# Attention with a top-32 mask and a mixture of experts: K and Q of two heads loaded and transposed together, V loaded in two groups, and a new order on every engine

## The chip, the cores and the metric

One NeuronCore of a Trainium2 chip runs the whole program. The metric is device time in microseconds; lower is better. Three runs of the kernel before took 1312.78, 1315.38 and 1315.54 us, and their median is the time before.

## The reference

Eight batches of eight heads, 576 positions, 64 values per head, in float32. Each row of scores keeps its 32 largest entries. The result feeds a mixture of eight experts.

```python
scores = scale * np.matmul(q, k.transpose(0, 1, 3, 2))
kth = np.partition(scores, -top_k, axis=-1)[..., -top_k:-top_k + 1]
scores = np.where(scores >= kth, scores, -1000000000.0)
attn = np.exp(scores - np.max(scores, axis=-1, keepdims=True))
attn = attn / (np.sum(attn, axis=-1, keepdims=True) + 1e-09)
attn_out = np.matmul(attn, v)
...
logits = x @ w_gate
...
h = np.maximum(x[mask] @ w1[e], 0.0)
out[mask] = h @ w2[e]
```

## The kernel before, in words

The attention stage goes over 32 pairs: eight batches, two heads at a time. `prep` brings a pair in, `tile_ops` and `soft` work on its nine tiles of 128 query rows (tile 4 holds the last 64 rows of both heads), `tail`, `values` and `logits` finish it. Several pairs are under way at a time. A mixture-of-experts stage follows, which the change leaves alone.

**Two halves.** The products run in 16-bit floats, so K and Q are each kept as a high and a low half in one buffer (`nk`, `nq`, two of each, used in turn). The high half is made on ACT (lines 349 and 350), the low half on POOL: a scaled copy (354), then the scaled copy less the high half (355). V is split likewise on POOL (342, 345, 346).

**What SP issues for a pair.** SP's queue issues all DMAs of the stage and takes them strictly in its own order. `loads` (lines 335 and 336) brings K, and again Q, in four DMAs: for each head its first 512 rows, then its last 64. `loadv` (340 and 341) does the same for V. `turn` (line 360) transposes one half of K or Q by a DMA, 9 blocks of 128 columns each: `K2`, `K3`, `Q2`, `Q1`, four DMAs.

**The row maxima.** After three tiles a small POOL instruction (`most`, line 462) puts the rows' maxima into a spare column of Q's second buffer half, and a DMA (`q2`, line 463) transposes those three blocks anew over the same place. So there are three such transposes in a pair: the first for tiles 0 to 2, the middle one for 3 to 5, the third for 6 to 8.

**Who reads the transposes.** `scores` (line 407) multiplies Q's halves with K's for a first pass, on which DVE finds the 32nd largest (lines 411 to 438) and ACT makes the masks (425, 443). `again` in `soft` computes the scores a second time, transposed: line 482 reads `K2` and `Q1`, line 483 `K3` and `Q2` with the maxima in it. So line 483 of tiles 3 to 5 needs the middle transpose of line 463. Line 487 is the exponential, 490 and 493 on POOL split its result into halves, 584 multiplies with V.

**What sets the order.** Every operation is handed to a planner (`Loom`) with a number from the table `TAU`, one per operation and tile, plus the pair's number times `PER`. On each engine the operations stand in the order of these numbers; a pair's later operations are dealt between the next pairs' earlier ones. SP is one of these engines, `e="D"`. A `pre` entry is a true dependence, an `order` entry only a place behind another. The planner's costs `d` and `late` don't change the order, which the table fixes. The first pair has a path of its own (`first`), and the last one its own numbers (names with `_`).

Of the kernel before, what the change touches and what calls it, by code (L numbers as in the profile page):

```python
# [190 lines left out]
def attention(tc, q,k,v,w_gate,x_out,L,acc,cuts, pairs,ahead=()):  # L191
    NCH=6
    nc=tc.nc
    CW=576//NCH; NCAND=8*NCH
    with ExitStack() as ctx:
# [31 lines left out]
        def rims():  # L227
# [9 lines left out]
        TAU=dict(s0=[0.7506526,1.3511746,1.8516096,8.2571781,10.1588313,11.5600494,16.7645738,18.766314,20.4677931],  # L237
            s1=[0.8507396,1.4512616,3.0526537,8.3572652,10.2589183,11.7602234,16.8646608,18.866401,20.6679671],
            c0=[-2.8733791,-1.2175335,1.996755,6.8668891,8.425332,10.568191,14.4642983,16.8019626,19.0422243],
            c1=[-2.6785738,-1.0227282,4.6266274,7.2564998,8.71754,12.3214393,15.9253385,17.9707948,19.139627],  # L240
            c2=[-1.4123389,0.6331174,4.431822,7.0616944,9.9837749,12.0292312,14.9513117,18.3604056,20.0162511],
            c3=[-1.3149362,0.3409094,4.139614,7.6461105,9.6915669,10.9578017,14.7565063,17.3863787,19.8214458],
            c4=[-2.1915603,-0.146104,3.6526006,7.1590971,10.0811776,12.2240366,15.8279358,18.5552109,19.4318351],
            c5=[-2.4837684,-0.3409094,3.3603925,7.7435132,9.3993588,11.2500098,16.2175466,18.7500163,20.3084592],
            k0=[-0.9253255,1.3149362,4.7240301,8.2305266,10.6655937,12.71105,16.5097546,19.3344324,20.5032646],
            k1=[-0.0487013,1.8019496,5.0162381,8.5227347,11.1526071,13.1980634,17.0941707,19.6266404,20.990278],
            k2=[0.4383121,2.3863657,5.1136408,9.1071508,11.4448151,13.4902715,17.4837814,19.9188485,21.0876807],
            k3=[0.7305201,3.4577952,5.7954596,9.4967615,12.1266339,13.5876741,18.0681975,20.1136538,21.282486],
            k4=[1.7045469,3.8474059,6.574681,9.8863722,12.418842,14.1720902,18.4578082,20.4058619,21.3798887],
            nt=[8.4307985,9.209026,13.1001638,19.3259842,21.1418485,23.2171219,26.8488505,29.4429423,30.4805791],  # L250
            sg=[8.6902077,11.0248903,14.3972097,20.1042117,22.1794852,23.4765311,27.3676689,29.9617607,30.7399883],
            fl=[4.5292247,5.6006542,7.4513052,11.5422178,13.9772849,15.2435197,20.6006672,21.4772914,21.8669021],
            o0=[4.8542199,7.3563951,9.2580482,13.2615285,16.1640518,17.3650959,22.5696203,24.0709254,24.9717085],
            o1=[5.0543939,7.4564821,9.3581352,14.1623116,16.2641388,17.6653569,23.6705774,24.1710124,25.0717955],
            y8=[4.8214328,6.6720837,8.0357213,13.2954661,14.3668956,16.3149492,21.5746941,21.6720967,22.4513182],
            rl=[11.5437087,14.6566189,16.7318923,22.9577128,23.9953495,25.5518046,30.9993974,31.2588066,32.8152617], mo=[7.2970843,16.7126769,24.7159306],
            q2=[6.355525,15.599925,24.844325], ma=[11.9603974,15.1631817,17.7654439,19.466923,20.7680541,23.7706644,29.1753628,26.9734486,30.8768419],
            mb=[12.4608325,15.4634427,17.9656179,19.667097,21.5687502,23.8707514,29.2754498,28.3746667,30.9769289],
            ag0=[12.7610935,15.8637907,18.466053,19.7671841,21.7689242,23.9708384,29.6757978,28.5748407,31.27719],
            ag1=[13.1614415,16.0639648,18.56614,20.3677061,22.0691852,24.6714474,29.7758848,28.7750148,31.377277],  # L260
            ag2=[13.4617026,16.3642258,18.966488,20.8681411,22.2693593,24.7715344,29.8759718,28.8751018,31.577451],
            ag3=[13.7619636,16.5643998,19.366836,21.0683152,22.3694463,24.8716215,30.0761459,29.0752758,32.077886],
            ex=[21.4012577,23.7359403,26.3300321,28.1458964,28.924124,32.2964434,35.1499444,34.3717168,38.0034454],
            eh=[21.8912528,24.2451509,25.1867102,25.6574898,0,30.8360657,37.4269806,33.6607435,44.0178954],
            el=[22.832812,28.011388,30.3652861,26.5990491,0,33.1899639,39.3100991,40.722438,44.9594546], cu=[46.3717935], tm=[27.4738837], tn=[27.6740577], ta=[27.7741447],
            tb=[27.8742317], te=[33.0746709], th=[31.3068454], tl=[31.777625], tc=[34.4799742], tr=[41.635174],
# [58 lines left out]
        def prep(n):  # L325
# [5 lines left out]
            def loads(nm,src,by=nc.sync):  # L331
                t=io.tile([128,9,64],F32,tag=nm+"n",name=nm+"n")
                for h in range(2):
                    o=(0,5)[h]
                    by.dma_start(out=t[:,o:o+4,:],in_=src[b,2*hp+h,0:512,:].rearrange("(p c) d -> p c d",c=4))
                    by.dma_start(out=t[64*h:64*h+64,4,:],in_=src[b,2*hp+h,512:576,:])
                nat[nm]=t
# [20 lines left out]
            def turn(nm):  # L358
# [3 lines left out]
                if nm=="Q2": P["Q2t"]=t  # L362
# [956 lines left out]
```

## Time and profile before

| | us |
|---|---|
| median of three runs | 1315.38 |
| the profiled execution's own time | 1316.4 |
| its span in the profile | 1314.6 |
| stretch 27 to 135, 135 to 862 (attention) | 108, 727 |
| stretch 862 to 1315 (experts) | 453 |
| PE busy over the span | 1230.4 (94%) |
| DVE busy | 1100.7 (84%) |
| ACT busy | 912.9 (69%) |
| POOL busy | 813.7 (62%) |
| DMA queue of SP, share of 16 engines | 42.9% |

How to read it: the busy shares are means over two stages of unlike make, so they don't tell what a change in one stage is worth. Instructions that only wait or issue a DMA are not busy time. The profiled execution took 1.0 us longer than the median. A DMA is shown twice in a trace: as the time that SP took to issue it, and as the time from issue to landing, when its readers may start.

### The profile page before, as it was taken

The page shows a single profiled execution, that of the slowest core. Times are in us where ns is not written, and L with a number is a line of the kernel's source. Part 1 is how long each engine was busy: PE and PEld are TensorE (multiplying, and loading weights), DVE is VectorE, ACT ScalarE, POOL GpSimd, SP SyncE. Part 2 cuts the span into 40 slices and gives each one's busy share as a digit, 9 for nine tenths or more (in the row PEclk, how much of TensorE's full clock was granted, in tenths as well). Part 3 has the DMA queues.
Part 4 walks back from the last instruction along what each step waited for, and adds up shares of the span by engine and source line. Part 5 has one row for each costly group of instructions (what it writes and reads, how often), then busy time and mean ns, then how long its engine had stood idle before and what let it go on. Part 6 is the DMA issues. An engine that isn't in the chain of part 4 may idle for free.

```text
span 1314.6 us, 43939 instructions
## 1 busy us (share of the span) xinstructions
PE 1230.4 (94%) x16447; PEld 937.3 (71%) x16448; DVE 1100.7 (84%) x5550; ACT 912.9 (69%) x2177; POOL 813.7 (62%) x1054
## 2 busy tenths in 40 slices
PE   8999999999999999999999999968999999999996
PEld 7777777787778777877777787757575665665662
DVE  7999989999999999999999999868999998843320
ACT  4989888998899989999898998714444353444220
POOL 3789788888888988899888988701213223311001
PEclk9999999999999999999999999968999999999998
DMA  5544645445544453653665364014557667672001
GB/s 109 105 90 82 128 95 101 113 103 95 128 81 104 109 115 89 103 139 78 99 134 96 77 140 87 20 47 155 179 186 237 185 157 205 196 201 76 21 17 38
DMA packets 317970, 148.60 MB, mean 113 GB/s; under 512 B 283444, under 2 KB 299828, under 8 KB 316724
## 3 DMA queue, kind: packets, MB, share of 16 engines
q1 hardware_dynamic: 311412, 126.55, 42.9%
q0 software_dynamic: 5888, 18.88, 4.6%
q8 instruction: 130, 2.13, 0.7%
q14 instruction: 92, 0.75, 0.2%
q10 hardware_dynamic: 448, 0.30, 0.1%
HBM read 71.34 MB, written 18.87 MB: 69 GB/s over the span
## 4 chain that ended last, share of the span: by engine, by line
PE 27%; DVE 24%; ACT 18%; issue 13%; DMA 11%; POOL 3%; SPq 1%; POOLq 0%; another core or an unknown queue 0%; ACTq 0%; DVEq 0%
DVE cd L411 8%; DMA Q<-nq 6%; ACT w L425 6%; PE ph L1179 5%; PE ph L1213 4%; DVE st L438 4%; PE pt L477 3%; PE s L428 3%; PE s L407 3%; ACT r L443 2%; PE pv L584 2%; ACT xb L558 2%; ACT F L487 2%; PE pt L483 2%; DMA wr<-in_moe_w_dram 2%
## 5 line engine op out<-in xcount | busy, mean ns | idle before, releaser
L411 DVE MAX8 cd<-s 128x8 f32<-128x96 f32 x1728 | 381.0, 250 | 24.9 <-PE s L407 24.0
L493 POOL TENSOR_TENSOR elm<-F,ehm 128x512 f16<-128x512 f32 x253 | 290.0, 1157 | 10.3
L438 DVE MAX8 st<-s 128x8 f32<-128x584 f32 x288 | 218.5, 768 | 18.2 <-PE s L428 17.0
L425 ACT ACTIVATE w<-s,st 128x576 uint16<-128x576 f32 x288 | 216.3, 751 | 5.8
L443 ACT ACTIVATE r<-s,st 128x576 bf16<-128x576 f32 x288 | 213.5, 753 | 1.2 <-DVE st L438 1.2
L483 PE MATMUL pt<-Q,K 65*128 65x128 f16 (+1 forms) x1280 | 186.2, 215 | 16.5 <-DMA Q<-nq 16.3
L407 PE MATMUL s<-K,Q 128*128 128x192 f16 (+3 forms) x1280 | 194.8, 288 | 3.9 <-DMA Q<-nq 2.8
L1179 PE MATMUL ph<-xT,w1h 128*128 128x288 f16 (+2 forms) x1056 | 191.6, 282 | 0.4 <-issue 0.4
L482 PE MATMUL pt<-Q,K 128*128 128x128 f16 (+1 forms) x1280 | 187.3, 214 | 0.0
L487 ACT ACTIVATE F<-pt 128x512 f32<-128x512 f32 x256 | 155.2, 608 | 18.3 <-PE pt L483 17.2
L1229 POOL DMA_INDIRECT out_dram<-ob,idx x39 | 40.2, 1031 | 203.7 <-ACT ob L1224 186.9
L428 PE MATMUL s<-w,off 128*128 128x384 f16 x576 | 151.7, 284 | 11.7 <-ACT w L425 3.1
L490 POOL TENSOR_SCALAR ehm<-F 128x512 f16<-128x512 f32 x253 | 155.2, 618 | 8.6 <-ACT F L487 8.6
L1179 PE MATMUL ph<-xT,w1l 128*128 128x288 f16 (+2 forms) x528 | 148.1, 282 | 0.0
L1133 POOL DMA_INDIRECT xg<-x,idx x40 | 46.9, 1173 | 150.4 <-DVE idx L1076 47.3
L482 PEld LDWEIGHTS <-K 128*128 128x128 f16 x1280 | 117.0, 98 | 31.3 <-issue 26.6
L584 PEld LDWEIGHTS <-ehm 128*128 128x128 f16 x2024 | 112.5, 98 | 15.1 <-issue 0.5
L483 PEld LDWEIGHTS <-K 65*128 65x128 f16 x1280 | 117.9, 98 | 4.1
L584 PE MATMUL pv<-vl,ehm 128*128 128x65 f16 x1012 | 118.9, 193 | 0.0
L584 PE MATMUL pv<-vh,ehm 128*128 128x65 f16 x1012 | 118.6, 194 | 0.1
L584 PE MATMUL pv<-vh,elm 128*128 128x65 f16 x1012 | 118.6, 193 | 0.0
L477 PEld LDWEIGHTS <-r 128*128 128x128 bf16 x1280 | 86.0, 97 | 42.8 <-issue 30.6
(297 smaller groups left out, 3370.1 us busy)
## 6 DMA issues: line engine op xcount, KB each, us to landing
wr<-in_moe_w_dram SPq DMA_DIRECT2D x32, 1024.0 KB, 6.8
kn<-in_k_dram SPq DMA_DIRECT2D x64, 128.0 KB, 2.7
vt<-in_v_dram SPq DMA_DIRECT2D x64, 128.0 KB, 2.8
x<-xb SPq DMA_DIRECT2D x8, 1024.0 KB, 5.0
qn<-in_q_dram SPq DMA_DIRECT2D x62, 128.0 KB, 2.3
Q<-nq SPq DMA_TRANSPOSE x160, 2.9
kn<-in_k_dram SPq DMA_DIRECT2D x64, 16.0 KB, 2.2
K<-nk SPq DMA_TRANSPOSE x64, 3.3
```

Source lines behind the costliest of these rows:

```text
L407: x=T.matmul(s_ps[rows,S0+a:S0+b_],P[Q][:,qc],P[K][:,h*576+a:h*576+b_],start=(Q=="Q1"),stop=(Q=="Q2"))
L411: x=V.max(D["cd"][:,c*8:c*8+8],D["s"][:,S0+CW*c:S0+CW*(c+1)])
L425: A.activation(D["w"],D["s"][:,S0:S0+576],AF.Sign,bias=P["st"][:,i,32:33],scale=(1+2.0**-21),accum_out=acc[:,col])
L428: x=T.matmul(D["s"][:,S0+a:S0+b_],off,P["w"][i][:,a:b_],start=False,stop=True,skip_group_check=True)
L438: def next8(): V.max(P["st"][:,i,24:32],D["s"][:,S0-8:S0+576])
L443: A.activation(r,D["s"][:,S0:S0+576],AF.Relu,bias=P["st"][:,i,31:32],scale=-1.0)
L482: T.matmul(o,K2[:,kb:kb+128],Q1[:,qc],start=False,stop=False,skip_group_check=True)
L483: T.matmul(o,K3[0:65,kb:kb+128],Q2[0:65,qc],start=False,stop=(c==3 and h==sub[-1][0]),skip_group_check=True)
L487: A.activation(D["E"],D["pt"],AF.Exp,scale=ESC)
L493: G.tensor_tensor(el,D["E"],D["eh"],op=ALU.subtract); P["e"][i]=(D["eh"],el)
L584: for m_ in (range(N-3) if part==0 else range(N-3,N)): T.matmul(out,seq[m_][0],seq[m_][1],start=(m_==0),stop=(m_==N-1))
L1179: P.matmul(B["ph"][:,lo-c0:hi-c0],a[:,c,fs],xT[:,b+c,lo:hi],start=(i==0),stop=(i==11),skip_group_check=True)
```

## The change

Four things. `loads` takes both heads in one DMA for the first 512 rows and one for the last 64, so K and Q need two DMAs each where they needed four. V's four DMAs stay, but the two large ones (`loadv`) and the two small ones (`loadw`) become two operations that may stand apart in SP's order. From the second pair on, K's halves lie in one tile `Kt` and Q's in one tile `Qt`, and one DMA transposes both halves, 18 blocks; the first pair keeps one DMA a half. The three transposes of the maxima stay as they are. Last, the whole table `TAU` has new numbers (two lines of it are shown), so that the operations of all engines are dealt out anew; some waits for the loads become places in the order.

```diff
-            q2=[6.355525,15.599925,24.844325], ma=[11.9603974,15.1631817,17.7654439,19.466923,20.7680541,23.7706644,29.1753628,26.9734486,30.8768419],
...
+            q2=[1.9066575,12.0754975,23.5154425], ma=[19.56701,22.6697073,25.0717955,26.8733616,28.0744057,30.1762329,37.6827585,34.7802352,38.7837156],
...
@@ -330,15 +330,14 @@
             nat={}
             def loads(nm,src,by=nc.sync):
                 t=io.tile([128,9,64],F32,tag=nm+"n",name=nm+"n")
-                for h in range(2):
-                    o=(0,5)[h]
-                    by.dma_start(out=t[:,o:o+4,:],in_=src[b,2*hp+h,0:512,:].rearrange("(p c) d -> p c d",c=4))
-                    by.dma_start(out=t[64*h:64*h+64,4,:],in_=src[b,2*hp+h,512:576,:])
+                both=bass.AP(tensor=t.tensor,offset=t.offset,ap=[list(t.ap[0]),[320,2],[1,256]])
+                by.dma_start(out=both,in_=src[b,2*hp:2*hp+2,0:512,:].rearrange("h (p c) d -> p h (c d)",c=4))
+                by.dma_start(out=t[:,4,:],in_=src[b,2*hp:2*hp+2,512:576,:])
                 nat[nm]=t
             def loadv():
-                for h in range(2):
-                    nc.sync.dma_start(out=vt[:,h,0:4,0:64],in_=v[b,2*hp+h,0:512,:].rearrange("(p c) d -> p c d",c=4))
-                    nc.sync.dma_start(out=vt[64*h:64*h+64,h,4,0:64],in_=v[b,2*hp+h,512:576,:])
+                for h in range(2): nc.sync.dma_start(out=vt[:,h,0:4,0:64],in_=v[b,2*hp+h,0:512,:].rearrange("(p c) d -> p c d",c=4))
+            def loadw():
+                for h in range(2): nc.sync.dma_start(out=vt[64*h:64*h+64,h,4,0:64],in_=v[b,2*hp+h,512:576,:])
             def highv(): G.tensor_scalar(vh[:,:,:,0:64],vt[:,:,:,0:64],VS,0.0,op0=ALU.mult,op1=ALU.add)
             def scaledv():
                 nat["vs"]=io.tile([128,2,5,64],F32,tag="vs",name="vs",bufs=1)
@@ -356,14 +355,18 @@
             def clean(): G.memset(nq[:,1,:,64:65],0.0)
             fl=lambda t: t.rearrange("p a b -> p (a b)")
             def turn(nm):
-                t=io.tile([128,9,128],F16,tag=nm,name=nm,bufs=2)
-                nc.sync.dma_start_transpose(t,fl({"Q1":nq[:,0],"Q2":nq[:,1],"K2":nk[:,0],"K3":nk[:,1]}[nm]))
-                P[nm]=fl(t)
-                if nm=="Q2": P["Q2t"]=t
+                w=nm[0]
+                if w+"t" not in P:
+                    t=P[w+"t"]=io.tile([128,2,9,128],F16,tag=w+"t",name=w+"t",bufs=2)
+                    for j in range(2): P[w+str(j+1+(w=="K"))]=fl(t[:,j])
+                    if w=="Q": P["Q2t"]=t[:,1]
+                t=P[w+"t"]; src=nq if w=="Q" else nk
+                if len(nm)==1: nc.sync.dma_start_transpose(t.rearrange("p a b c -> p (a b) c"),src.rearrange("p a b c -> p (a b c)"))
+                else: j=int(nm[1])-1-(w=="K"); nc.sync.dma_start_transpose(t[:,j],fl(src[:,j]))
             prev=Ps.get(n-1); old=Ps.get(n-2); o3=Ps.get(n-3)
 
             p2=[old["done3"]] if old else []; p3=[o3["done"]] if o3 else []
-            o2=([prev["lds"]] if prev else [])+([old["q2r"]] if old else [])
+            o2=[old["q2r"]] if old else []
             def first():
 
                 lk=at((0,"",0),lambda: loads("k",k),e="D",d=2.2,late=2.0); l=at((0,"",0),lambda: loads("q",q,nc.scalar),e="A",d=2.9,late=2.4)
@@ -375,19 +378,19 @@
                 c=at((0,"",0),lambda: turn("Q2"),[h2],e="A",d=1.4,late=2.0); c=at((0,"",0),lambda: turn("Q1"),[c,q2],e="A",d=1.4,late=2.0)
                 P["ready"]=at((0,"",0),lambda: None,[c,b_]); P["q2r"]=q2
                 wipe=at((0,"",0),rims,[q2],e="V",d=1.3)
-                P["lds"]=at((0,"",0),loadv,[b_,wipe],e="D",d=2.2,late=2.0); at((0,"",0),gates,[P["lds"]],e="D",d=3.2,late=2.0)
+                lv=at((0,"",0),loadv,[b_,wipe],e="D",d=1.2,late=2.0); P["lv"]=lw=at((0,"",0),loadw,[],order=[lv],e="D",d=1.2,late=2.0); P["lds"]=at((0,"",0),lambda: None,[lv,lw]); at((0,"",0),gates,[P["lds"]],e="D",d=3.2,late=2.0)
                 a=at((0,"",0),highv,[P["lds"]],e="G",d=.69)
                 a=at((0,"",0),scaledv,[a],e="G",d=.7); P["vready"]=at((0,"",0),lowerv,[a],e="G",d=1.39)
             if n==0: first(); return
             def go(name,*a,**kw): return at((n,name,0),*a,**kw)
-            lk=go("ldk",lambda: loads("k",k),o2,e="D",d=2.25,late=2.0); l=go("ldq",lambda: loads("q",q),[lk],e="D",d=2.3,late=2.0)
+            lk=go("ldk",lambda: loads("k",k),o2,order=[prev["lv"]],e="D",d=1.15,late=2.4); l=go("ldq",lambda: loads("q",q),[],order=[lk],e="D",d=1.15,late=2.4)
             h1=go("hk",lambda: high("k"),[lk]+p2,e="A",d=1.055); s1=go("gk",lambda: scaled("k"),[lk,prev.get("lk")],e="G",d=.643); P["lk"]=k2=go("lk",lambda: lower("k"),[h1,s1],e="G",d=1.24)
             h2=go("cq",clean,p2,e="G",d=.07)
             h2=go("hq",lambda: high("q"),[l,h2]+p2,e="A",d=1.055); s2=go("gq",lambda: scaled("q"),[l,prev.get("lq")],e="G",d=.643); P["lq"]=q2=go("lq",lambda: lower("q"),[h2,s2],e="G",d=1.24)
-            a=go("tk2",lambda: turn("K2"),[h1]+p2,e="D",d=1.34,late=1.53); b_=go("tk3",lambda: turn("K3"),[a,k2],e="D",d=1.34,late=1.53)
-            c=go("tq2",lambda: turn("Q2"),[b_,h2],e="D",d=1.34,late=1.53); c=go("tq1",lambda: turn("Q1"),[c,q2],e="D",d=1.34,late=1.53)
-            P["ready"]=c; P["q2r"]=q2
-            P["lds"]=go("ldv",loadv,[l]+p3,e="D",d=2.66,late=2.0)
+            b_=go("tk",lambda: turn("K"),[h1,k2]+p2,e="D",d=1.55,late=1.6)
+            c=go("tq",lambda: turn("Q"),[h2,q2],order=[b_],e="D",d=1.55,late=1.6)
+            P["ready"]=at((n,"",0),lambda: None,[b_,c]); P["q2r"]=q2
+            lv=go("ldv",loadv,p3,order=[l],e="D",d=1.22,late=2.4); P["lv"]=lw=go("ldw",loadw,[],order=[lv],e="D",d=1.22,late=2.4); P["lds"]=at((n,"",0),lambda: None,[lv,lw])
             a=go("hv",highv,[P["lds"]],e="G",d=.69)
             s3=go("gv",scaledv,[P["lds"],prev["vready"]],e="G",d=.69); P["vready"]=go("lv",lowerv,[a,s3],e="G",d=1.39)
         def tile_ops(P,i):
```

On SP, from a pair's first maxima transpose (the first row) to its middle one, with the loads of later pairs between them (`vt`, `kn`, `K` are V, K as loaded and K transposed; `nq_193` is this pair's Q buffer). Before:

```order
L463 DMA_TRANSPOSE Q_3664<-nq_193 128x3x128
L360 DMA_TRANSPOSE K_4183<-nk_190 128x9x128
L340 DMA vt_198<-in_v_dram 128x4x64
L341 DMA vt_198<-in_v_dram 64x64
...
L360 DMA_TRANSPOSE K_4315<-nk_190 128x9x128
L463 DMA_TRANSPOSE Q_3664<-nq_193 128x3x128
```

And in the change, to the third one:

```order
L466 DMA_TRANSPOSE Qt<-nq_188 128x3x128
L340 DMA vt_201<-in_v_dram 64x64 x2
L334 DMA kn<-in_k_dram 128x2x256
L335 DMA kn<-in_k_dram 128x1x64
L334 DMA qn<-in_q_dram 128x2x256
L335 DMA qn<-in_q_dram 128x1x64
L466 DMA_TRANSPOSE Qt<-nq_188 128x3x128
L364 DMA_TRANSPOSE Kt<-nk_195 128x18x128
L364 DMA_TRANSPOSE Qt<-nq_193 128x18x128
L466 DMA_TRANSPOSE Qt<-nq_188 128x3x128
```

Where the dots are, the two V loads stand a second time, for the other head. Both K transposes and the large V loads have left the place before the middle transpose; loads of K and Q and the small V loads stand there now, and the transposes of 18 blocks come behind it.

On POOL, from the middle maxima (`st`) to the lower half of the next pair's Q (`nq<-scq`). Before:

```order
L462 TENSOR_SCALAR nq0_188<-st_6796 128x3
L490 TENSOR_SCALAR ehm_7913<-F_7688 128x512
L493 TENSOR_TENSOR elm_7929<-F_7688,ehm_7913 128x512
L354 TENSOR_SCALAR scq_7955<-qn_7462 128x576
L507 TENSOR_SCALAR cuts_146<-st_6074 128x2x9
L355 TENSOR_TENSOR nq1_193<-scq_7955,nq1_193 128x9x64
```

And in the change, where line 462 has become 465, 490 and 493 are 493 and 496, 342 is 341, 354 and 355 are 353 and 354:

```order
L465 TENSOR_SCALAR nq0_188<-st_6671 128x3
L496 TENSOR_TENSOR elm_7762<-F_7547,ehm_7688 128x512
L354 TENSOR_TENSOR nk1_195<-sck_7601,nk1_195 128x9x64
L341 TENSOR_SCALAR vh2_205<-vt2_204 128x10x64
L353 TENSOR_SCALAR scq_7851<-qn_6933 128x576
L493 TENSOR_SCALAR ehm_7870<-F_7757 128x512
L493 TENSOR_SCALAR ehm_7879<-F_7838 128x512
L354 TENSOR_TENSOR nq1_193<-scq_7851,nq1_193 128x9x64
```

The lower half of Q, which the transpose of `Qt` reads, stands two rows later, and the lower half of K, which stood ahead of the middle maxima, now stands behind them.

## Rows read from the trace of the kernel before

**Rows 1.** Windows view: stretch, its length, busy us by engine, clock, DMA share, GB/s.
```profile
core 0: us, PE busy (x) PEld busy (x) DVE busy (x) ACT busy (x) POOL busy (x), PEclk, DMA share, GB/s
313.00:339.00 26.00, 23.00 (x376) 19.04 (x377) 23.04 (x137) 22.17 (x57) 21.33 (x29) 1.00 0.59 94
417.00:443.00 26.00, 25.47 (x427) 20.88 (x428) 25.14 (x148) 24.33 (x63) 23.59 (x32) 1.00 0.42 94
```
**Rows 2.** List of waits: who waited for what, us in total, times, longest.
```profile
PE pt L483 <- DMA Q<-nq: 16.3, 14, 2.2
PEld L407 <- DMA Q<-nq: 4.0, 6, 0.9
```
**Rows 3.** Timeline of ACT: start us, length, line and operation; K scaled, once a pair.
```profile
24.37 1.17 ACT L350 ACTIVATE nk<-kn 128x1152 f16<-128x1152 f32 x1 [0.15 <-DMA kn<-in_k_dram]
...
261.71 1.16 ACT L350 ACTIVATE nk<-kn 128x1152 f16<-128x1152 f32 x1
...
312.38 1.16 ACT L350 ACTIVATE nk<-kn 128x1152 f16<-128x1152 f32 x1
339.93 1.16 ACT L350 ACTIVATE nk<-kn 128x1152 f16<-128x1152 f32 x1
...
806.48 1.16 ACT L350 ACTIVATE nk<-kn 128x1152 f16<-128x1152 f32 x1
```
**Rows 4.** Timeline of POOL, SP and PE, a pair whose middle maxima came late.
```profile
317.38 0.20 POOL L462 TENSOR_SCALAR nq<-st 128x3 f16<-128x3 f32 x1 [1.69 <-PE s L428]
320.15 1.33 SPq L360 DMA_TRANSPOSE K<-nk  x1
321.58 2.04 SPq L463 DMA_TRANSPOSE Q<-nq  x1
325.01 0.22 PE L483 MATMUL pt<-Q,K 65*128 65x128 f16 x1 [2.11 <-DMA Q<-nq]
```
**Rows 5.** Timeline of POOL and SP, first and middle maxima where no wait follows.
```profile
283.64 0.20 POOL L462 TENSOR_SCALAR nq<-st 128x3 f16<-128x3 f32 x1
283.88 1.20 SPq L463 DMA_TRANSPOSE Q<-nq  x1
291.90 0.20 POOL L462 TENSOR_SCALAR nq<-st 128x3 f16<-128x3 f32 x1 [1.50 <-PE s L428]
294.37 1.19 SPq L463 DMA_TRANSPOSE Q<-nq  x1
```
**Rows 6.** View of line 463, all its transposes (3 blocks).
```profile
DMA to landing us min/median/max: 2.3/2.3/4.8
```
**Rows 7.** View of line 360, K's and Q's transposes together (9 blocks).
```profile
DMA to landing us min/median/max: 2.8/3.0/6.6
```
**Rows 8.** Groups of POOL, 135 to 785 us: busy us, mean ns of one.
```profile
L493 POOL TENSOR_TENSOR elm<-F,ehm 128x512 f16<-128x512 f32 x200 | 229.3, 1157 | 8.4
L490 POOL TENSOR_SCALAR ehm<-F 128x512 f16<-128x512 f32 x200 | 122.6, 618 | 0.0
...
L355 POOL TENSOR_TENSOR nq<-scq,nq 128x576 f16<-128x576 f32 x25 | 32.0, 1281 | 0.0
...
L342 POOL TENSOR_SCALAR vh<-vt 128x640 f16<-128x640 f32 x25 | 18.2, 729 | 0.0
...
L354 POOL TENSOR_SCALAR scq<-qn 128x576 f32<-128x576 f32 x25 | 16.8, 671 | 0.0
```
**Rows 9.** Timeline of POOL and PE: middle maxima, and scores that waited for Q.
```profile
732.68 0.20 POOL L462 TENSOR_SCALAR nq<-st 128x3 f16<-128x3 f32 x1 [1.49 <-PE s L428]
744.79 0.67 PE L407 MATMUL s<-K,Q 128*128 128x192 f16 x4 [0.47 <-DMA Q<-nq]
```
**Rows 10.** Timeline of POOL at the start: K of the first pair.
```profile
5.70 1.15 POOL L370 TENSOR_SCALAR nk<-kn 128x1152 f16<-128x1152 f32 x1 [1.38 <-DMA kn<-in_k_dram]
```
**Rows 11.** The page's queues and DMA issues: KB each, median us to landing.
```profile
q1 hardware_dynamic: 311412, 126.55, 42.9%
...
vt<-in_v_dram SPq DMA_DIRECT2D x64, 128.0 KB, 2.8
...
vt<-in_v_dram SPq DMA_DIRECT2D x64, 16.0 KB, 2.7
```

146 lines of the change are left out of this document (73 added, 73 removed).

## The prediction

> **What bounds the kernel now.** I read the stages first. The attention stage is about 860 of the 1315 us; the change touches nothing behind it. The windows view shows the same 26 us twice: in one pair every engine works nearly all the time (PE 25.47, DVE 25.14 of 26 us), in another all five lose 2 to 2.5 us together [rows 1]. One common stall, then, and no engine that is slower than the rest. The list of waits names it: PE's largest wait on a DMA is line 483 (score products of the second pass, which read Q's half with the row maxima) for a Q transpose, 16.3 us in 14 waits; next come the scores at line 407, 4.0 us in 6, 0.9 of them at the very start [rows 2].
>
> The pace agrees. ACT scales K of each new pair once, so those instructions are a clock: 30 periods from 24.37 to 806.48 us, 26.07 us each; the two from 261.71 to 312.38 hold no such wait and last 25.34; the next lasts 27.55 [rows 3]. So 30 x (26.07 - 25.34) = 22 us are lost; the waits alone give 16.3 + 4.0 - 0.9 = 19.4. I take 21 us as what late transposes cost.
>
> Which transpose, and why late? Three per pair bring the maxima (L463). Where no wait follows, the first is issued 0.04 us after its POOL instruction ends (283.84 to 283.88), but the middle one at 294.37, 2.27 us after its own (292.10) [rows 5]. In the late pair it is issued 4.0 us after (317.58 to 321.58), because SP, which issues in order, is busy with the K transpose ahead; PE starts at 325.01 after 2.11 us idle, so it needed the data at 322.90, 5.32 us after the POOL instruction [rows 4]. All waits at L483 that I followed were for the middle one. A small transpose lands 2.3 us after issue at best and in the median, 4.8 at worst [rows 6]. So the margin is 5.3 - 2.3 - 2.3 = 0.7 us now: any delay of SP by a microsecond stops PE.
>
> **The change, part by part.**
> 1. *Queue order, middle transpose.* In the new order no K transpose and no large V load stand between the first and the middle transpose, only two V tails and four loads that wait for nothing recent. They take SP 1.2 us (first transpose) + 6 issues of about 0.6 = 4.8 us, so from 283.88 SP would be free at 288.7, 3.4 us before the POOL instruction ends at 292.10 [rows 5]. Then the middle transpose goes out at once, as the first does now, and its margin is 5.3 - 2.3 = 3.0 us; even the worst landing, 4.8, fits. Gain: all 16.3 us of waits, with what they cost beside them.
> 2. *Q's two transposes as one.* It needs the lower half of Q, a POOL instruction, and stands later there. Behind the middle maximum POOL now runs one L490, one L493, one L354, a short one and the lower half, 3.9 us; in the new order L493 1.157, the lower half of K about 1.28, L342 0.729, L354 0.671, twice L490 0.618 and the lower half of Q 1.281, together 6.35 us [rows 8]. The scores of the next pair need it 11.4 us after the maximum (732.88 to 744.32, where PE was held up) [rows 9]. That leaves 11.4 - 6.35 - 0.1 = 4.95 us for the landing. No row shows a transpose of 18 blocks. Lower bound: one of 9 blocks, 3.0 in the median; upper: twice that, 6.0, with 6.6 the worst of any [rows 7]. 3 blocks take 2.3 and 9 take 3.0, so 0.117 us a block and 4.05 for 18; I take that, since the two sizes are of the same instruction. Margin 0.9 us, hardly more than the 0.7 the middle one has now. But here SP is idle before it, so only the scatter of landings remains, not SP's lateness: I take 5 us of waits over 31 pairs, a third of what the middle one cost. Bounds 0 and 10.
> 3. *K's two as one.* Ready 2.4 us behind the maximum, landing by 6.6: 5 us early. Nothing.
> 4. *The third maximum transpose* follows the large Q transpose, as it follows one now, and never made PE wait. Nothing to 1 us, in the 5 above.
> 5. *Loads.* Eight DMAs for twelve: four issues of about 0.6 us fewer per pair on a queue that is not the bound once part 1 holds; already counted.
> 6. *Start.* Two issues fewer before K of the first pair has landed, which POOL waits for until 5.70 [rows 10]: 0 to 1.5 us, I take 1.0, as DVE has other work then.
> 7. *The order on PE, DVE, ACT* is dealt anew with the same instructions. The pace between stalls, 25.34, I leave as it is: 0, bounds -1.5 and +6 us (0.2 per pair).
>
> Sum against the profiled execution: 1316.4 - 21 + 5 - 1.0 = 1299.4. The median shown is 1.0 below that execution, so I forecast **1298 us**.
>
> A rule speaks against part 2. The Trainium skill, page "DMA: Bandwidth & Descriptors", section "Latency and other measured facts", gives DMA transposes 261 GB/s where the middle dimension isn't contiguous, and its "Anatomy of one DMA" a fixed 2.0 us. An estimate from both for 128x18x128 halves (590 KB) is 2.0 + 2.3 = 4.3 us instead of 4.05, and the sum by it would be about 1300. For 3 and 9 blocks the same estimate gives 2.4 and 3.1, where this trace has 2.3 and 3.0.
>
> **The rivals.**
> *A. The large Q transpose is late in every pair (slower).* Place: PE's first scores of a pair, L407 in the old numbering. It decides from a landing of 4.95 us; each further 0.1 us costs 31 x 0.1 = 3.1 us, and the 22 us are used up at about 5.65. At 6.0, twice the 9 blocks: 31 x 1.05 = 33 against 22, so about 1326. For it: POOL's order leaves only 0.9 us. Against: 3 to 9 blocks added 0.7 us, not 2. 6 in 100.
>
> *B. The new tail loads clog the middle transpose (slower).* Their source is written as two blocks of 64 rows. If a DMA is dealt out by that outer count, two engines take 64 rows each instead of sixteen taking 4. A packet on this queue takes 0.429 x 16 x 1314.6 us / 311412 = 29 ns in the mean, so 1.9 us per tail and 3.7 for two, ahead of the middle transpose on those engines. From about 287 to 297.4, when PE needs it, there are 10 us: it decides from 80 ns a row. At 100 ns it would cost 2.5 us in each pair, 31 x 2.5 - 22 = +55, about 1370. Against: large V loads carry 8 times the rows of the V tails (128 KB to 16) and land at 2.8 against 2.7 us [rows 11]. 3 in 100.
> The page named above says in "Why a DMA increments its semaphore by 16 and not by 1" that the count of engines is the largest up to 16 that divides the slowest dimension of both sides, which would be two here. No run yet shows it.
>
> *C. Half of the stalls stay.* SP's issues are held up from time to time whatever they are (2.04 us for 1.2 at 321.58 [rows 4]), and hit the Q transposes or the third maximum, whose margins are about a microsecond: 10 to 12 us given back, about 1306. For it: the waits of line 407 today are of this kind [rows 2]. 13 in 100.
>
> *D. Nothing comes of it:* PE meets another limit as soon as the transposes are in time, in a new order that runs slower between stalls by as much. Against: pairs without the wait keep 25.34 us now. 1313 to 1318; 5 in 100.
>
> **How the numbers follow.** The forecast has 73 in 100, and its own range is 1290 (all 22 us gone, 1.5 at the start, 1.5 in the new order) to 1304 (10 us left instead of 5). C lies above it, and the range runs to **1309** to take it in; A, B and D are left out with part of the tails, about 2 in 10. 0.2% is 2.6 us, about what a measurement of this kernel can tell from no change. Faster: the forecast, C and a piece of A, 0.88. Same: D, 0.05. Slower: the rest of A and B, 0.07.
>
> **What would show it.** Right: no wait of the second score pass on the maxima's transpose, the middle one issued within 0.1 us of its POOL instruction; a median landing of the 18-block transposes near 4 us; waits of the first scores for them of some 5 us in all; a pace near 25.5 us; about 15 fewer us from the start to the last pair. Wrong: waits of the scores for Q above 10 us in total (A, C), middle transposes landing over 4.8 us after issue (B), or a pace without waits that isn't 25.3 to 25.4 (D).

## The result, and the profile after

The change took 1299.78 us in the median of four runs (1297.84 to 1301.71), the kernel before 1314.08 beside it (1310.91 to 1315.54): a ratio of 0.9902, 95% interval 0.9878 to 0.9925. The profiled execution took 1298.74 us, its span is 1297.0. So 1298 was forecast and the run lies inside the range. The steps did not come out as well as the sum, as the rows show.

The windows view, cut at the first and the last of ACT's K scalings [rows 3] and at DVE's last instruction of the attention stage, gives 30 periods and the rest. Columns as in [rows 1]. Before:

```profile
24.37:806.48 782.11, 742.20 (x12117) 608.76 (x12117) 733.61 (x4267) 705.75 (x1774) 678.09 (x894) 1.00 0.51 104
806.50:867.80 61.30, 56.20 (x900) 46.42 (x896) 46.01 (x254) 44.32 (x115) 39.81 (x51) 0.98 0.22 50
```

After:

```profile
24.56:791.03 766.47, 731.68 (x12041) 608.99 (x12041) 729.58 (x4271) 702.50 (x1775) 675.01 (x895) 1.00 0.47 106
791.03:849.64 58.61, 54.00 (x891) 45.77 (x887) 45.87 (x253) 44.09 (x115) 38.60 (x49) 1.00 0.22 48
```

Of the 17.6 us that the span lost, the 30 periods gave 782.11 - 766.47 = 15.6 (25.55 us each instead of 26.07), the last pair 2.7; the start took 0.2 more (24.37 to 24.56), and what follows attention 0.6 more.

The list of waits answers to [rows 2]: the row of the second score pass (L483 before, L486 now) is gone, and the first scores still wait for Q.

```profile
PEld L410 <- DMA Qt<-nq: 3.6, 9, 0.8
```

0.57 us of it is at the very start, so 3.0 in eight pairs. The timeline of POOL, SP and PE shows one of these pairs, and the counterpart to [rows 4] in it: the middle maxima end at 309.66, and their transpose goes out at 309.68.

```profile
309.45 0.21 POOL L465 TENSOR_SCALAR nq<-st 128x3 f16<-128x3 f32 x1 [1.63 <-PE pv L587]
309.68 2.22 SPq L466 DMA_TRANSPOSE Qt<-nq  x1
312.03 1.94 SPq L364 DMA_TRANSPOSE Kt<-nk  x1
314.47 1.28 POOL L354 TENSOR_TENSOR nq<-scq,nq 128x576 f16<-128x576 f32 x1
315.77 3.49 SPq L364 DMA_TRANSPOSE Qt<-nq  x1
```

In all 32 pairs the middle one is issued within 0.03 us of its POOL instruction's end (0.03 to 4.0 before). Here Q's large transpose took SP 3.49 us to issue, and the scores of the next pair waited 0.18 us (until 321.29), so Q landed 5.5 us after its issue.

One row speaks against the change: the shortest period. The first of the 30 (24.87 us in the change) is left out of this, here and in the table below. Before, the windows of undisturbed pairs go down to 25.14 us; in the change to 25.35, with DVE as busy as ever. Before, then after:

```profile
572.50:597.64 25.14, 24.60 (x412) 20.23 (x410) 24.27 (x143) 23.46 (x60) 22.81 (x31) 1.00 0.42 97
```
```profile
100.22:125.57 25.35, 24.24 (x410) 20.34 (x407) 24.22 (x144) 23.43 (x62) 22.67 (x31) 1.00 0.40 96
```

### The profile page after: what moved, and what is told of

It is laid out like the page before. It is cut to its first block, busy times and chain, and to the rows that moved or that the text cites. A ratio compares the mean times of both kernels' runs of the same rounds, so it can differ in the third digit from the quotient of the medians.

```text
span 1297.0 us, 43401 instructions
## 1 busy us (share of the span) xinstructions
PE 1218.3 (94%) x16367; PEld 937.1 (72%) x16368; DVE 1096.2 (85%) x5550; ACT 909.5 (70%) x2177; POOL 809.1 (62%) x1054
## 4 chain that ended last, share of the span: by engine, by line
DVE 40%; PE 25%; issue 12%; ACT 10%; DMA 8%; POOL 3%; SPq 1%; POOLq 0%; another core or an unknown queue 0%; ACTq 0%; DVEq 0%
DVE cd L414 14%; DVE st L441 8%; PE ph L1182 5%; ACT w L428 4%; DMA Qt<-nq 4%; PE ph L1216 3%; PE pv L587 3%; PE pt L480 3%; PE s L431 3%; DVE cd L422 2%; DVE cd L420 2%; PE s L410 2%; DVE st L419 2%; DMA wr<-in_moe_w_dram 2%; DVE st L421 1%
## 5 line engine op out<-in xcount | busy, mean ns | idle before, releaser
L414 DVE MAX8 cd<-s 128x8 f32<-128x96 f32 x1728 | 375.1, 249 | 11.2 <-PE s L410 9.6
L441 DVE MAX8 st<-s 128x8 f32<-128x584 f32 x288 | 217.9, 766 | 16.8 <-PE s L431 15.7
L428 ACT ACTIVATE w<-s,st 128x576 uint16<-128x576 f32 x288 | 217.3, 755 | 5.8
L410 PE MATMUL s<-Kt,Qt 128*128 128x192 f16 (+3 forms) x1280 | 194.0, 286 | 8.0 <-ACT r L446 5.3
L486 PE MATMUL pt<-Qt,Kt 65*128 65x128 f16 (+1 forms) x1280 | 185.2, 214 | 0.0
L485 PE MATMUL pt<-Qt,Kt 128*128 128x128 f16 (+1 forms) x1280 | 185.1, 214 | 0.0
L485 PEld LDWEIGHTS <-Kt 128*128 128x128 f16 x1280 | 117.7, 98 | 27.5 <-issue 22.8
L486 PEld LDWEIGHTS <-Kt 65*128 65x128 f16 x1280 | 117.3, 98 | 10.2
L480 PE MATMUL pt<-out__180,r 128*128 128x128 bf16 (+1 forms) x1280 | 111.2, 213 | 8.8 <-ACT xb L561 4.2
L1182 PEld LDWEIGHTS <-w1h 128*128 128x128 f16 x1056 | 97.5, 98 | 28.0 <-issue 3.7
```

Of the source, the lines that this page charges most:

```text
L410: x=T.matmul(s_ps[rows,S0+a:S0+b_],P[Q][:,qc],P[K][:,h*576+a:h*576+b_],start=(Q=="Q1"),stop=(Q=="Q2"))
L414: x=V.max(D["cd"][:,c*8:c*8+8],D["s"][:,S0+CW*c:S0+CW*(c+1)])
L428: A.activation(D["w"],D["s"][:,S0:S0+576],AF.Sign,bias=P["st"][:,i,32:33],scale=(1+2.0**-21),accum_out=acc[:,col])
L441: def next8(): V.max(P["st"][:,i,24:32],D["s"][:,S0-8:S0+576])
L485: T.matmul(o,K2[:,kb:kb+128],Q1[:,qc],start=False,stop=False,skip_group_check=True)
L486: T.matmul(o,K3[0:65,kb:kb+128],Q2[0:65,qc],start=False,stop=(c==3 and h==sub[-1][0]),skip_group_check=True)
```

## The experiments

Three explanations fit so far: SP's order (the middle transpose is no longer behind a waiting K transpose), fewer and larger DMAs, or the new order of all engines. Eleven kernels, the change once more among them, were run in three groups; each group shared one chip with the kernel before. The table gives them together: median, ratio to the kernel before, then of the profiled execution the first K scaling, the 30 periods' sum, the shortest period, and the time from the last K scaling to the end of attention.

| run | median us | ratio (95%) | first | 30 periods | shortest | last |
|---|---|---|---|---|---|---|
| before | 1314.1 | | 24.37 | 782.1 | 25.14 | 61.3 |
| change | 1299.8 | 0.9902 (0.9878 to 0.9925) | 24.56 | 766.5 | 25.35 | 58.6 |
| change again | 1298.5 | 0.9911 (0.9884 to 0.9937) | 24.98 | 765.9 | 25.33 | 58.6 |
| e1 | 1295.0 | 0.9881 (0.9852 to 0.9910) | 24.35 | 762.6 | 25.33 | 58.6 |
| e2 | 1295.4 | 0.9879 (0.9849 to 0.9908) | 24.29 | 763.0 | 25.14 | 60.6 |
| e3 | 1372.9 | 1.0472 (1.0433 to 1.0511) | 24.64 | 838.5 | 26.72 | 59.9 |
| e4 | 1300.5 | 0.9923 (0.9893 to 0.9952) | 24.30 | 765.4 | 25.34 | 59.7 |
| e5 | 1294.1 | 0.9832 (0.9785 to 0.9878) | 24.40 | 756.5 | 25.13 | 60.5 |
| e6 | 1297.7 | 0.9843 (0.9800 to 0.9887) | 24.84 | 763.4 | 25.34 | 59.4 |
| e8 | 1292.6 | 0.9817 (0.9776 to 0.9859) | 24.48 | 756.6 | 25.13 | 61.8 |
| e9 | 1290.3 | 0.9842 (0.9817 to 0.9867) | 23.63 | 755.8 | 25.12 | 60.5 |
| e10 | 1296.7 | 0.9895 (0.9858 to 0.9931) | 24.54 | 760.6 | 25.12 | 60.6 |
| e11 | 1299.4 | 0.9904 (0.9866 to 0.9942) | 24.66 | 762.1 | 25.33 | 61.4 |

The kernel before had a median of 1311.65, 1318.2 and 1311.11 us in the three groups (e1 to e4; e5, e6, e8; the rest). So medians of different groups are compared by their ratios, and small differences by the stretches of the profiles. There is one profile of each kernel; the change's two differ by 0.6 us in the 30 periods, and what follows attention, which no edit touches, takes 446 to 451 us in all of them. The last column also holds the granted clock: it is 1.00 of full speed there in both runs of the change, e1, e2, e5, e9 and e10, and 0.96 to 0.98 in the others.

**e2, SP's order alone.** Three places of the table of the kernel before:

```diff
-tk3=[-13.288825] ldv=[-14.444375] tk3_=[-10.977725]
+tk3=[-9.5]       ldv=[-18.5]      tk3_=[-9.5]
```

> The kernel before with three entries of SP's order changed and nothing else: the V loads ahead of the first K transpose, the second K transpose behind the middle transpose of the maxima. All 19 DMAs of a pair stay. Our theory: the middle transpose is issued within 0.3 us of its GpSimd instruction in most pairs (1.6 to 4.0 us before), the waits of the second score pass for transposes fall from 16.3 us to under 3, the pace falls from 26.07 to 25.4 to 25.7 us and the time to 1298 to 1306 us; the lower Q transposes are issued about a microsecond later than before, which may give up to 5 us back at the first scores. Rival (fewer DMAs and merged transposes): 1310 to 1315. Rival (the new order of all engines): 1311 to 1316, since the other engines' order is untouched.

1295.37 us, a little under the range expected: the whole gain of the change, with all 19 DMAs a pair of the kernel before and the other engines' order as before. The middle transpose goes out at once, as this timeline of POOL and SP shows; the V loads stand ahead, the second K transpose behind.

```profile
309.12 0.20 POOL L462 TENSOR_SCALAR nq<-st 128x3 f16<-128x3 f32 x1 [1.69 <-PE s L428]
309.35 1.18 SPq L463 DMA_TRANSPOSE Q<-nq  x1
310.59 1.35 SPq L360 DMA_TRANSPOSE K<-nk  x1
```

PE's second score pass waits for no transpose any more; the first scores wait 2.9 us in 4 (4.0 in 6 before, [rows 2]). Two long periods, 27.25 and 28.13 us, keep the mean at 25.43. In the second the first scores waited 1.4 us for Q; then the granted clock fell for a while to the lower level, 1.2 GHz (0.50 of full speed from 525 to 527 us), and the period's mean is 0.94 where the next has 1.00:

```profile
506.30:534.43 28.13, 26.28 (x412) 21.43 (x410) 24.72 (x143) 23.43 (x61) 22.83 (x31) 0.94 0.46 83
```

Both rivals, which expected 1310 and more, are out as the main cause.

**e3, the wait put back.** In the change, K's transpose ahead of the middle one:

```diff
-tk=[-5.7199725]
+tk=[-13.6]
```

> The change with one entry altered: K's 18-block transpose stands ahead of the middle transpose of the maxima on SP. It waits for the lower K of GpSimd, which comes right behind the maxima there. Our theory: the middle transpose is issued 3.5 to 4.5 us after its GpSimd instruction, of which the second score pass has about 3.0 us to spare (5.3 less 2.3 of landing), so it waits some 1 to 1.7 us in every pair: pace 26.5 to 27.2 us, time 1330 to 1352 us. Rivals (fewer DMAs, or the order of the other engines): no change, 1298 to 1302.

1372.92 us, more than expected. The sign and place were right: the middle transpose is issued 4.45 us after its POOL instruction in the median, and the list of waits has the row back.

```profile
DVE cd L414 <- PE s L410: 67.9, 46, 4.0
...
PE pt L486 <- DMA Qt<-nq: 45.0, 30, 2.9
```

45.0 us in 30 is 1.5 a pair, as expected. But see the landing in the chain of waits: a middle transpose issued between K's and Q's large ones took 3.84 us until PE had it, not 2.3 [rows 6] (2.9 in the median of the 30).

```profile
285.14 3.84 DMA Qt<-nq
```

And the 30 periods grew by 838.5 - 766.5 = 72 us, 2.4 a pair: what I priced was the wait's row, and that is less than the wait costs. DVE, held up by the scores that stand behind the waiting matmul on PE, idles 67.9 us for them, 9.6 in the change. A smaller part is the clock. Seven of the 30 periods have a mean granted clock of 0.94, the rest 1.00. Two neighbours with nearly the same wait (2.17 and 2.21 us) show the price in the windows view:

```profile
135.39:163.75 28.36, 25.28 (x421) 21.05 (x418) 24.40 (x145) 23.59 (x62) 22.70 (x31) 1.00 0.36 86
163.75:193.08 29.33, 26.37 (x425) 22.60 (x422) 24.35 (x144) 23.65 (x62) 22.75 (x31) 0.94 0.54 123
```

The seven last 29.5 us in the mean, the seven others with a wait over 2 us 28.5: about 1 us each, some 7 of the 27 us by which the periods grew more than the rows.

**e1, the transposes split again.** The change's order, with K's and Q's halves as two DMAs each in the same place:

```diff
-lambda: turn("K")
+lambda: (turn("K2"),turn("K3"))
-lambda: turn("Q")
+lambda: (turn("Q2"),turn("Q1"))
```

> The change's order, but K's and Q's transposes of pairs 1 to 31 are again two DMAs of 9 blocks each. If the order of SP is what gave the time (our theory), the middle transpose of the maxima is still issued within 0.1 us of its GpSimd instruction in most pairs, nothing returns at the second score pass, and the time stays at 1297 to 1302 us; SP issues 2 x 1.3 us for a turn in place of 2.0, so the last transpose of the maxima may be issued 0.6 us later, within its room. If fewer and larger DMAs are what gave it (rival), the pace goes back towards 26 us per pair and the time to 1308 to 1314 us.

1295.04 us, better than either theory had it. The first scores wait for Q in the first two pairs only, and the pace falls to 25.42. Its 30 periods are 3.9 us shorter than the change's: that is what merging costs where the transposes stand. K's and Q's were split together, so the run doesn't part them; but the waits that went were for Q.

**e4, one tail DMA per head again** (in every pair):

```diff
-by.dma_start(out=t[:,4,:],in_=src[b,2*hp:2*hp+2,512:576,:])
+for h in range(2): by.dma_start(out=t[64*h:64*h+64,4,:],in_=src[b,2*hp+h,512:576,:])
```

> The change with the 64 tail rows of K and Q loaded by one DMA per head again (two more DMAs per load, in every pair). If the two-head tail is slow because it is cut in two parts only (our reading of the 4.8 us it took at the start), the first pair's K tails land within 2.8 us of issue, GpSimd's first K instruction starts at 5.4 to 5.9 us (6.34 in the change) and the first scores at 15.0 to 15.6 us (15.93); the rest of the time stays, 1298 to 1300 us in all. Rival (the start is late for another reason, such as both queues being shared): first scores still at 15.8 to 16.0 us.

1300.48 us. At the start K's loads go by SP's queue and Q's by ACT's. In the change the chain of waits (start, length, what) has the first K tail landing 4.79 us after issue, where 16 KB tails took 2.2 in the median before:

```profile
1.38 4.79 DMA kn<-in_k_dram
```

With a tail per head POOL starts on K at 5.33 us instead of 6.34, as expected; the first scores at 15.68 instead of 15.93, less than expected: three quarters of the microsecond are lost again, as Q's last transpose lands 4.6 us after its issue (11.03) instead of 4.0 (11.92). Timelines of POOL and PE, the change, then e4:

```profile
6.34 1.15 POOL L373 TENSOR_SCALAR nk<-kn 128x1152 f16<-128x1152 f32 x1 [2.02 <-DMA kn<-in_k_dram]
15.93 0.75 PE L410 MATMUL s<-Kt,Qt 128*128 128x192 f16 x5 [0.40 <-DMA Qt<-nq]
```
```profile
5.33 1.27 POOL L373 TENSOR_SCALAR nk<-kn 128x1152 f16<-128x1152 f32 x1 [1.01 <-DMA kn<-in_k_dram]
15.68 0.50 PE L410 MATMUL s<-Kt,Qt 128*128 128x192 f16 x3 [0.31 <-DMA Qt<-nq]
```

This run also shows what no row before could: when transposes of 18 blocks (L364, K's and Q's) land, and how long SP is busy with one.

```profile
L364 SPq DMA_TRANSPOSE Kt<-nk x31: 1748/1971/3614, 32.9 to 797.5; - x31
L364 SPq DMA_TRANSPOSE Qt<-nq x31: 1747/2045/3777, 36.6 to 799.9; - x31
...
DMA to landing us min/median/max: 3.9/4.5/5.8
```

**e6, the lower half of Q earlier on POOL.**

```diff
-lq=[-32.7191843] hv=[-36.0146417]
+lq=[-34.84]      hv=[-33.2]
```

> The change with one GpSimd step moved: the lower half of Q comes ahead of V's upper half and of two upper halves of exponentials, so Q's 18-block transpose can be issued 1.5 to 1.8 us earlier. If the waits of the first scores (3 us in 8 pairs) and the long periods come from Q's late landing, the waits fall under 0.5 us, and the time by 2 to 4 us against the change, 1295.5 to 1298 us. If the long periods have another cause (the transpose's issue holding up SP), they stay: 1298.5 to 1301 us.

1297.74 us. Beside the start, 0.7 us of waits are left (2.3 in 3, of which 1.6 at the start), a little more than expected, and the 30 periods are 3.1 us shorter than the change's. The long periods of the change (the 25th, 26.61, and the 5th, 25.97) went with the waits; the 17th stayed (26.24, now 26.13), with one of the waits that are left.

**e5, the change's DMAs in the order before.** The new `loads`, `loadw` and `turn`, the old table, and by hand on SP:

```diff
-tk2=[-17.911025] tk3=[-13.288825] tq2=[-8.666625] tq1=[-1.733325] ldv=[-14.444375]
+tk=[-9.5] tq=[-8.6] ldv=[-18.5] ldw=[-18.4]
```

> The DMA parts of the change (merged K and Q loads, V loads in two groups, one transpose each of K and Q) with the order that PE, ACT, DVE and GpSimd had before; SP's order by hand: V loads ahead, both large transposes behind the middle transpose of the maxima, Q's ahead of the K loads. Our theory, as the two runs with the order before and with split transposes left it: the shortest and usual period of that order is 25.15 to 25.25 us (25.35 to 25.45 in the change), GpSimd makes the lower Q some 2 us earlier in it, so no first score waits for Q: pace 25.2 to 25.4 us, time 1288 to 1295 us. Rival (the merged transposes themselves cost): periods of 25.4 and more and waits of the first scores as in the change, 1297 to 1302 us.

Both numbers came: 25.14 us in undisturbed pairs and 25.22 in the mean, 1294.1 us. The windows view of one such pair and of the 30 periods:

```profile
99.41:124.56 25.15, 24.62 (x412) 20.24 (x410) 24.29 (x143) 23.48 (x60) 22.80 (x31) 1.00 0.44 96
...
24.40:780.90 756.50, 737.05 (x12074) 603.23 (x12073) 730.18 (x4269) 703.23 (x1774) 677.54 (x894) 1.00 0.50 107
```

**e8, the same with split transposes** (the edit of e1 on e5).

> As the run with the change's DMA parts and the order before, but K's and Q's transposes are two DMAs of 9 blocks each. If merging the transposes costs (they issue 2.0 us in one piece and land 4.1 us or more after, against the two of 1.3 us each), this one is 1 to 4 us faster than the merged one; if merging only matters where Q is late, both are within 1.5 us of each other, 1288 to 1295 us. Against the run that changed SP's order alone (1295.4), what is left of a difference is the K and Q loads in two DMAs.

756.6 against 756.5 us in 30 periods, 1292.6 against 1294.1 in the median. Merging is worth nothing where Q isn't late, and costs where it is. Against e2, which has the same order on the other four engines, the two long periods are gone. Its K and Q loads are four DMAs a pair fewer, but its transposes also have other places on SP, so which of the two did it is open.

**e10 and e11, whose order costs the 0.2 us?** e10 is the change with the old order on PE, DVE and ACT; e11 has the new order on these three and the old one on POOL, with SP as in e5. Of e10's edit, which takes the old numbers for every operation of the three engines, two lines:

```diff
-s0=[7.8568301,8.3572652,10.3590053,15.8637907,18.0657049,19.166662,24.0709254,25.5722305,27.4738837],
+s0=[0.7506526,1.3511746,1.8516096,8.2571781,10.1588313,11.5600494,16.7645738,18.766314,20.4677931],
...
-c0=[0.5357148,3.2629898,6.3798757,10.7629964,13.7824795,15.7305331,19.2370297,21.0876807,22.3539155],
+c0=[-2.8733791,-1.2175335,1.996755,6.8668891,8.425332,10.568191,14.4642983,16.8019626,19.0422243],
...
```

> The change, with its new order on GpSimd and SP kept, and the order before on PE, DVE and ACT. Theory: the undisturbed period of the change is 25.35 us and not 25.14 because of what PE, DVE and ACT do in the new order (DVE is busy 24.2 us in either, and idle 1.13 us in place of 0.86), so here it returns to 25.14 to 25.2 and the pace to 25.2 to 25.4: 1290 to 1296 us. Rival (GpSimd's new order costs it): the undisturbed period stays at 25.35 and the time at 1297 to 1301.

> The counterpart: the change with the new order on PE, DVE and ACT, and the order before on GpSimd, SP by hand as in the run with the change's parts. Theory: undisturbed period 25.35 us as in the change, pace 25.4 to 25.55, 1295 to 1300 us, and the last pair as short as in the change (58.6 us from its first instruction on ACT to the end of attention). Rival: 25.14 to 25.2 us.

The shortest period goes with these three engines: 25.12 in e10, 25.33 in e11. The mean of e10 is 25.35, its median 1296.69 us, just above the range: the first scores wait 1.4 us for Q beside the start, since POOL's new order makes the lower Q late, and the period with the longest of these waits lasts 27.32 at a mean clock of 0.94. The last pair of e11 took 61.4 us, not 58.6; its mean granted clock there is 0.96, not 1.00. The windows view of e11:

```profile
24.66:786.79 762.13, 730.20 (x12040) 608.16 (x12040) 728.66 (x4271) 701.32 (x1775) 677.54 (x893) 1.00 0.49 107
786.79:848.14 61.35, 56.47 (x898) 47.80 (x894) 45.96 (x253) 44.17 (x115) 39.69 (x51) 0.96 0.20 52
```

**e9 and the change side by side.** e5 with tails per head in the first pair alone:

```diff
-by.dma_start(out=t[:,4,:],in_=src[b,2*hp:2*hp+2,512:576,:])
+for h in range(2 if n==0 else 0): by.dma_start(out=t[64*h:64*h+64,4,:],in_=src[b,2*hp+h,512:576,:])
+if n: by.dma_start(out=t[:,4,:],in_=src[b,2*hp:2*hp+2,512:576,:])
```

> The change's DMA parts with the order before and SP's order by hand, and in the first pair alone the tails of K and Q by one DMA per head. The pace stays at 25.2 us; first K instruction of GpSimd at 5.3 to 5.7 us, first scores 0.1 to 0.4 us earlier than without (15.9): 1290 to 1294 us, 5 to 9 us under the change on the same chip.

> The change itself, run again beside the three others on one chip, so that they are compared with it and not only with the kernel before: 1297 to 1302 us, pace 25.5 to 25.6 us, first scores of some 8 pairs waiting for Q.

The pace is 25.19 us, and the first scores start at 15.15, earlier than expected. On one chip e9 took 1290.31 us (1289.10 to 1291.95, six runs) and the change 1298.45 (1297.36 to 1301.70, six runs): 8.1 us, and the runs don't overlap. It has the lowest median of this study, though e5 and e8, in another group, have ratios of 0.9832 and 0.9817 to its 0.9842 and can't be told apart from it. Windows view of e9:

```profile
23.63:779.39 755.76, 736.76 (x12074) 603.17 (x12074) 729.71 (x4269) 703.00 (x1774) 677.37 (x893) 1.00 0.49 107
```

## Why the prediction was right, point by point

**The cause was right.** The stall was SP's order, one transpose behind a K transpose that waited for POOL. e2 removes it with three numbers and has the whole gain; e3 puts it back and loses 72 us in the periods. What showed it beforehand was the row of waits [rows 2] together with the issue time in [rows 4].

**What set off each wait was another thing than I wrote.** With a landing of 2.3 us I had a margin of 0.7 us, which any further lateness of SP would use up. But the 14 transposes that PE waited for were issued 1.6 to 4.0 us after their maxima (median 2.0), no later than the others (1.8 to 3.0, median 2.3, the last two pairs left out). They landed later: PE had them 3.3 to 4.8 us after issue (median 4.3), where the recorded landings of the others took 2.3 to 3.1. Three of the 14 in the chain of waits before (start, length, what):

```profile
346.55 4.39 DMA Q<-nq
372.61 4.75 DMA Q<-nq
476.30 4.20 DMA Q<-nq
```

So SP's order takes about 2 us of the 5.3 that there are, and a landing over some 3.2 us does the rest. Issued at once, even the worst landing fits; in e2 the recorded ones still run from 2.4 to 4.0, and nobody waits. What makes some of them slow was not tried.

**Part 1, 21 us, was too small.** The old order without late transposes runs 756.5 us for 30 periods (e5), against 782.1 before: 25.6 us. SP's order alone (e2) gave 19.1 of it; nearly all the rest lies in e2's two long periods (24.66 and 25.14 in e5), and what keeps those away in e5 is open. I read the pace between stalls from two periods [rows 3], 25.34 us in the mean, but even these were not free of SP's lateness: e2, where only SP's places differ, needs 25.15 and 25.22 for the same two. And the waits' 19.4 us are only what PE's rows show; e3 showed 45 us of rows for 72 of time. Here too a part is the clock: the two longest periods before, 27.83 and 27.94 us, have a mean of 0.94.

**Part 7, the new order at 0, was too small by nearly as much.** It costs 762.1 - 756.5 = 5.6 us (e11 against e5), and 766.5 - 760.6 = 5.9 in the change itself (against e10), at the upper of the bounds I gave, +6. By the shortest period it is 0.2 us a pair on PE, DVE and ACT together.

**Part 2, 5 us for Q's large transpose, was about right:** 766.5 - 762.1 = 4.3 us against e11, which has POOL's old order and SP's by hand, and 3.9 against e1. The lower half of Q was ready 6.1 us after the maximum (6.35 in the sum) and SP issued the transpose at once, so what was left was the scatter of landings, as I had it: in the eight pairs that waited, Q landed 5.5 to 6.3 us after its issue, where 4.95 were left. What I didn't look at is SP's own time, 2.0 us to issue 18 blocks where 9 took 1.3 [rows 4]; but only in four of the eight was it long (3.3 to 3.6), in the other four it was the usual 1.8 to 2.2. The landing's median is 4.5 us for K's and Q's together in e4 (18 of 62 are recorded), above the 4.05 I took and within 3.0 to 6.0; Q's nine alone have 4.1. By the figures of the Trainium skill's page "DMA: Bandwidth & Descriptors" in "Latency and other measured facts" and "Anatomy of one DMA" 4.3 us was estimated; the 2.0 us in the latter are given for DMAs that GpSimd issues, and these are SP's. It lies between the two medians, so the trace agrees with it about as well as with 4.05.

The three terms give -25.6 + 5.6 + 4.3 = -15.7, and the periods moved by -15.6. That they meet is no proof, since they are steps of one chain of runs (before, e5, e11, change); what bears out the parts is e10 and e1, which stand beside it. My own terms were -21 + 0 + 5 = -16. **So the sum was right because two errors cancelled,** and only the experiments could tell. One reading was loose as well, though nothing rests on it: of the five engines, PEld lost 1.8 us, not 2 to 2.5 [rows 1].

**Part 6, the start, had the wrong sign** (+0.2 to the first K scaling instead of -1.0, and the first scores 0.3 later). The step that failed is that two issues fewer bring K in earlier: the one tail of both heads lands 4.8 us after issue, and POOL starts 0.6 us later [rows 10]. e4 and e9 show that the tail in one piece does it: POOL starts at 5.33 and 5.37 us with a tail per head.

**Not foreseen: the last pair,** -2.7 us. Where the granted clock is 1.00 in that stretch, it takes 58.6 us with the new order (change, e1) and 60.5 to 60.6 with the old one on PE, DVE and ACT (e2, e5, e9, e10), so the order gives 1.9; the rest goes with the clock, 0.98 before. POOL's new order alone doesn't do it (e10). The new order of the three alone doesn't seem to, either: 25 us into the last pair, at a clock of 1.00, e11 already has PE, DVE and ACT less busy than the change. Windows view of 5 us, the change, then e11:

```profile
816.03:821.03 5.00, 4.97 (x117) 4.36 (x114) 4.94 (x36) 4.20 (x16) 3.32 (x4) 1.00 0.10 23
```
```profile
811.79:816.79 5.00, 4.16 (x101) 3.56 (x98) 4.00 (x27) 3.90 (x14) 4.83 (x7) 1.00 0.29 64
```

I had given the last pair no term.

**The rivals.** A and C fell: 3.0 us of waits for Q, not 10 and more. B fell as a clog: no wait at L486, and the middle transposes stay in time. Its premise was seen at the start, though: the tail of two blocks takes 4.8 us to land, a tail per head 2.9 in the median of e4. The DMA packets in the traces show why: the first pair's K and Q tails are 256 packets of 256 bytes, which run from 3.94 to 5.86 us in the change, never more than four at a time, and from 3.54 to 4.22 in e4, up to 17 at a time. The Trainium skill's page "DMA: Bandwidth & Descriptors" has in "Why a DMA increments its semaphore by 16 and not by 1" a count of engines that divides the slowest dimension of both sides. Four at a time for two such DMAs agrees with its two engines each. What it costs here is a quarter (e4) to three quarters (e9 against e5, 15.15 and 15.90) of a microsecond at the first scores, once: with a tail per head in every pair (e4) the 30 periods are only 1.1 us shorter. D was a quarter right: a new limit, 0.2 us a period.

**Left open.** Why the new order's period is 0.2 us longer is settled to three engines and no further. In the change DVE's fill waits for ACT's masks (L443 for L428) for 0.16 us a period in the middle of the stage; but in e11 that row almost vanishes and the period is the same. Why SP takes 3 to 4 us for some large transposes was not tried.

## What to carry to other kernels

A queue that issues in order passes on every wait: list what stands ahead of the transfer that PE waits for, and ask what that one waits for. Try first to move those few places alone; here three numbers gave all that a new table and new DMAs gave, and the new table cost 6 us in the periods that nobody saw because it came with the gain. Look at the landing of each transfer that was waited for, too, and not only at the median of all: a place in the queue leaves room or it doesn't, but the slow landings decide when that shows. Read the pace without stalls from the shortest periods, not from the ones that hold no listed wait, and count the time of a wait by the periods, since the rows of waits showed three quarters of it before (19.4 of 25.6 us) and less in e3 (45 of 72). Read the granted clock of each period beside it.

## What the hardware showed beside this

- SP is busy 1.2 us with the issue of a DMA transpose of 3 blocks, 1.3 with 9 and 2.0 with 18 (medians before and in the change); in e5 one of 18 blocks took it up to 4.1; a plain load takes it 0.5 to 0.6 in the median.
- A transpose of 3 blocks, 2.3 us from issue to landing in the median before [rows 6], took 3.3 to 4.8 in the 14 cases that PE waited for, each of them issued right behind a K transpose.
- A load whose source is two blocks of 64 rows landed 4.8 us after issue at the start of the change; with a DMA for each block POOL could start 1.0 us earlier.
- The granted clock fell within attention in pairs in which PE had waited: mean 0.94 in the 28.13 us period of e2, the 27.32 us one of e10 and seven of e3, at about 1 us each in e3.
- In e11 the granted clock fell while the last pair was still at work: its last 17.30 us have a mean of 0.87 of full speed, and the 24.90 us behind it 0.50, the lower level, 1.2 GHz. How much of the pair's 61.4 us is the clock is open, since it was behind before.
